# A memory-attention and mixture-of-experts kernel: copies moved to ScalarE, background work in one more place of each step, and two earlier loads of the last weights

## The chip, the cores and the metric

One core of one Trainium2 chip. The metric is the device time of one execution in microseconds (us); lower is better. The kernel before took 598.34 us (median of three executions, 596.36 to 599.28). Differences of up to about 0.5% are what such a measurement can't tell from no change.

## The reference

Inputs are float32: q, k, v of 4 batches x 8 heads x 576 tokens x 64, phi with 32 memory slots, weights of a dense mixture of 4 experts (w1 512x1024, w2 1024x512 each) and of a soft mixture of 8 experts with 4 slots each (called v1 and v2 in the kernel, phi2 for the slots).

```python
a = softmax(phi, axis=tokens)                       # 576 tokens -> 32 memory slots, per head
k_m, v_m = a.T @ k, a.T @ v                         # 32 x 64 per head
x = softmax(q @ k_m.T / 8, axis=-1) @ v_m           # -> (2304, 512)
p = domain_probs / domain_probs.sum(-1)
x = sum_e p[:, e] * (relu(x @ w1[e]) @ w2[e])       # 4 experts, all tokens
logits = x @ phi2                                   # (2304, 32)
d = softmax(logits, axis=0); c = softmax(logits, axis=1)
slots = d.T @ x                                     # 32 slots x 512
out = c @ (relu(slots_e @ v1[e]) @ v2[e] for 8 experts)   # (2304, 512)
```

## The kernel before, in words

The order of all instructions is written by hand: each engine executes its queue in the order in which the Python code issues them. The name in front of an arrow is the tile that an instruction writes, the names behind it are what it reads.

**Units and steps.** A unit is one batch (the last batch is cut in two). A unit has 8 steps n, one for each half of an expert's w1. A step has 8 products `up` (4 blocks fb x 2 halves ki of the tokens): 6 matmuls into one of two banks `mm` (L434 to L436, hi and lo parts of A and g), a relu by ScalarE into `hT` (L444) and, after the second half, a transposition by VectorE into `h` (L446). A holds the attention weights in two parts, hi and lo; g is w1 with v_m multiplied in (`g_mult`, L391), hi part by ScalarE (L401), lo part by VectorE (L402), one step ahead. `logits` (L461) multiplies hT by M, which is w2 @ phi2. So that w2 need not be applied per token, M is made in unit 0: in each step four `flip`s (four transpositions of a 128x512 piece of w2 into a bank, L488, copied out in two halves, L493 and L494), `part` (L500, L505) and `fold` (L510, copied to M at L514).

**The order within a step.** After each product comes a place, `at` = 0 to 7. `logits` of the step before stand at `at_l` = 0, `g_mult` of the next step at `at_g` = 2, its two output halves at `at_c` = 3 and 4. At all places but `at_g`, `pump` takes one entry from the list fg (softmax statistics, the token sums L625, row softmax of the unit before) and one from the list bg (`attention` of the next batch); an entry in `heavy` keeps bg waiting. In the first step of unit 0 the list `early` still finishes the attention of batch 0.

**`attention(b)`** lists loads and stages: kvs[0], kvs[1] (VectorE maxima of phi, L159), kvs[2] (transposes of them, L172), kvs[3] (subtractions), kvs[4] (exp on ScalarE), kvs[5], kvs[7] (VectorE sums, L207), kvs[6], kvs[8] (k times a), kvs[9] (the sums' matmuls, L243), kvs[10] (kbd, the blocks of keys, L266), kvs[11], kvs[12], kvs[13] (v times a), and for each of five token tiles scores (L315), exp, normalisation (L335 to L338) and transposition into A (L346 to L352). `shares` (L821, 20 small copies at L826 and L830) spreads domain_probs into `pe`.

**The end.** 160 blocks of 256 KB (32 of w2, 64 of v1, 64 of v2) pass through buffers that the main part no longer needs: `fill` loads n blocks into one buffer of a pool, `done` loads the next ones when they are used up. All loads are issued by SyncE, in order, about 8 in flight. Buffers: 5 blocks in those of the attention, 9 in each of five `big`, 4 each in A0, A1, two `raw`, two `g`. `raw`, one `g` and A0 hold h of the last unit until the last token sums (L625) are done.

Of the kernel before, what the change touches and what calls it, by code (L numbers as in the profile page):

```python
# [16 lines left out]
def kernel(  # L17
# [66 lines left out]
    vb = [const.tile([128, 128], F32, name=f"vb{n}") for n in range(2)]  # L84
    M = const.tile([128, 4 * NCH, NSLOT], F32)
    srun = const.tile([128, 8, 4, 32], F32)
# [62 lines left out]
    def kv_stages(b):  # L149
# [110 lines left out]
        def s5():  # L260
            t4 = bank()
            nc.tensor.transpose(
                t4[:, 0:128], st["km"].rearrange("p c d -> p (c d)"), ident
            )
            for c in range(2):
                nc.vector.tensor_copy(  # L266
                    out=kbd[b % 2][64 * c:64 * c + 64, :, c, :],
                    in_=t4[64 * c:64 * c + 64, 0:128].rearrange("p (i m) -> p i m", i=4),
                )
# [196 lines left out]
    def m_stages(n):  # L466
# [13 lines left out]
        def flip(a):  # L480
            def g():
# [11 lines left out]
                nc.scalar.copy(out=dst[0], in_=src[:, 0:2])  # L493
                nc.vector.tensor_copy(out=dst[1], in_=src[:, 2:4])  # L494
            return g
# [11 lines left out]
        def fold():  # L507
            t = bank()
            for a in range(4):
# [3 lines left out]
                )  # L513
            nc.vector.tensor_copy(  # L514
                out=M[:, 4 * n:4 * n + 4], in_=t[:, 0:128].rearrange("p (a s) -> p a s", a=4)
# [7 lines left out]
    def group(u):  # L523
# [69 lines left out]
        def weights(h):  # L593

            def f():
# [3 lines left out]
                we = st["we", h] = pc.tile([128, nt, 2, 32], F32, tag="we", bufs=2, name="we")  # L599
                for e in range(2):  # L600
                    nc.vector.tensor_tensor(
                        out=we[:, :, e], in0=st["dt"], in1=share(2 * h + e), op=ALU.mult
                    )
                if h == 1:
# [134 lines left out]
    with tc.manual_schedule():  # L739
# [96 lines left out]

        def pump():


            f = fg.pop(0) if fg else None  # L840
            if f:
                f()
            if f in heavy:
                return
            f = bg.pop(0) if bg else None
            if f:
                f()

        def attention(b):

# [9 lines left out]
            def with_q(f, m):  # L860
# [4 lines left out]
                return g  # L865
            items = [lambda: (load_phi(b), load_kv(b, 0)), lambda: load_kv(b, 1), kvs[0], kvs[1]]
            items += [kvs[2], None, kvs[3], lambda: load_q(b, 0), kvs[4]]
            items += [lambda: (load_q(b, 1), kvs[6]()), kvs[5], kvs[8], kvs[7], kvs[9], kvs[11], kvs[10]]
            items += [with_q(qs[0][0], 2), kvs[12], None, kvs[13]]
            for t in range(5):  # L870
# [14 lines left out]
        def finish(lu, n):  # L885
# [13 lines left out]
            if lu < NU - 3:  # L899
                bg.extend([None] * 8 + attention(lu + 2))  # L900

        for n, us in steps:
# [14 lines left out]
            if us == (0,) and n == 0:  # L917
                bg += attention(1)
                bg.insert(8, shares)
            if n == 0 and us[0]:  # L920
# [9 lines left out]
            if us == (NU - 2,) and n == NCH - 1:  # L930
                fill(bigp, "big", 9)
            if us == (NU - 1,) and n == MIX:
                for _ in range(4):
                    fill(bigp, "big", 9)
            gs = []
            for at, (u, fb, ki) in enumerate(ups):
                up(u, n, fb, ki)
                if at in at_c and gs:
                    gs.pop(0)()
                if at == at_l:  # L940
                    for lu, ln in last:
# [5 lines left out]
                if at == at_g and s + 1 < NG and us != (NU - 1,):  # L947
                    gs = g_mult(s + 1)
                else:
                    pump()  # L950
                if us == (0,):
# [11 lines left out]
        groups[lu][0](ln // 2)  # L963
        fill(const, "A1", 4, again=False)

        g_ = groups[lu][1]
# [7 lines left out]
        for _ in range(2):  # L974
            fill(rawp, "raw", 4)
        for _ in range(2):
            fill(gp, "g", 4)
        fill(const, "A0", 4, again=False)
# [242 lines left out]
```

## Time and profile before

| What | Value |
|---|---|
| Times of three executions | 599.28, 598.34, 596.36 us |
| The profiled execution's own time | 600.98 us |
| Its span | 599.1 us |
| Mean granted TensorE clock | 0.981 |
| TensorE matmul busy | 551.8 us (92%) |
| VectorE busy | 313.4 us (52%) |
| ScalarE busy | 204.2 us (34%) |
| Bytes moved by DMA | 106.22 MB |

Busy time is an average over stages. From about 40 to 505 us the four batches run through TensorE; from about 505 us on the blocks of the last weights stream in. Idle time of an engine counts only where the next step waits for it; "issue" as a releaser means that the profile shows none.

### The profile page before, as it was taken

To read this page: it belongs to the slowest core of one execution; us is meant where nothing else is said; L and a number is where in the kernel's file an instruction comes from. 1 tells how busy PE (TensorE), PEld (TensorE's weight loads), DVE (VectorE), ACT (ScalarE), POOL (GpSimd) and SP (SyncE) were. 2 spreads that over 40 slices of the span, in tenths; PEclk is the share of its full clock that TensorE was granted. 3 is DMA by queue.
4 is the path that set the end of the run, shared out by engine and by line. 5 is a ranking of instruction groups with operands and counts; after the bars stand their busy time and mean duration, and the time that the engine had idled before them with its cause. 6 is when DMAs were issued, how large, how long until landed. Compare 5 with 4: busy or idle time off the path is not lost.

```text
span 599.1 us, 15721 instructions
## 1 busy us (share of the span) xinstructions
PE 551.8 (92%) x6810; PEld 390.6 (65%) x6810; DVE 313.4 (52%) x693; ACT 204.2 (34%) x509; POOL 28.3 (5%) x34
## 2 busy tenths in 40 slices
PE   8887999999999899999989999999989998999993
PEld 7675778777776668877657787766557685324342
DVE  5656646864581566677345677761567362012022
ACT  2332445444451244554123344530444130102022
POOL 0000000101000001100000101000010000000000
PEclk9989999999999889999998899999999999999998
DMA  8992455444141733332446232440550398999998
GB/s 216 317 317 72 159 160 167 142 141 142 71 148 46 234 94 102 102 124 71 121 132 197 81 105 72 130 170 4 174 196 0 120 369 300 361 355 388 360 352 279
DMA packets 92771, 106.22 MB, mean 177 GB/s; under 512 B 30752, under 2 KB 55840, under 8 KB 92704
## 3 DMA queue, kind: packets, MB, share of 16 engines
q1 hardware_dynamic: 92704, 105.24, 54.2%
q8 instruction: 53, 0.87, 0.6%
q14 instruction: 14, 0.11, 0.1%
HBM read 100.50 MB, written 4.72 MB: 176 GB/s over the span
## 4 chain that ended last, share of the span: by engine, by line
PE 65%; DVE 14%; DMA 11%; issue 4%; ACT 3%; SPq 1%; POOL 0%; ACTq 0%; DVEq 0%; POOLq 0%
PE mm L434 11%; DMA v<-in_moe_w_dram 11%; PE at L625 9%; PE mm L436 9%; PE mm L435 9%; PE lb L461 6%; PE at L391 5%; DVE g L402 3%; PE at L315 3%; DVE h L446 2%; PE at L488 2%; PE mm L767 2%; PE at L299 1%; PE at L223 1%; ACT hT L444 1%
## 5 line engine op out<-in xcount | busy, mean ns | idle before, releaser
L444 ACT ACTIVATE hT<-mm 128x288 f32<-128x288 f32 x256 | 105.1, 411 | 235.0 <-PE mm L436 204.2
L446 DVE STREAM_TRANSPOSE h<-hT 128x576 f32<-128x576 f32 (+1 forms) x160 | 104.0, 652 | 138.6 <-ACT hT L444 126.8
L434 PE MATMUL mm<-A,g 128*128 128x288 f32 x512 | 170.4, 333 | 2.1 <-ACT g L401 1.0
L436 PE MATMUL mm<-A,g 128*128 128x288 f32 x512 | 153.2, 299 | 2.6 <-DVE g L402 2.6
L435 PE MATMUL mm<-A,g 128*128 128x288 f32 x512 | 152.6, 298 | 0.8 <-DVE A L352 0.8
L434 PEld LDWEIGHTS mm<-A,g 128*128 128x128 f32 x512 | 98.0, 191 | 48.9 <-ACT hT L444 20.4
L436 PEld LDWEIGHTS mm<-A,g 128*128 128x128 f32 x512 | 97.8, 191 | 3.9 <-DVE g L402 3.9
L435 PEld LDWEIGHTS mm<-A,g 128*128 128x128 f32 x512 | 98.3, 192 | 1.3 <-DVE A L352 1.0
L625 PE MATMUL at<-h,we 32*32 32x256 f32 x2304 | 58.3, 385 | 6.3 <-issue 4.4
L625 PEld LDWEIGHTS at<-h,we 32*32 32x32 f32 x2304 | 34.7, 103 | 25.5 <-issue 10.7
L402 DVE TENSOR_TENSOR g<-at,g 128x512 fp32r<-128x512 f32 x64 | 42.5, 671 | 5.5 <-ACT g L401 5.3
L461 PE MATMUL lb<-hT,M 128*32 128x288 f32 x512 | 40.8, 425 | 1.6 <-DVE M L514 1.6
L401 ACT CAST g<-at 128x512 fp32r<-128x512 f32 x64 | 37.2, 583 | 0.0
L391 PE MATMUL at<-raw,vb 64*32 64x512 f32 x512 | 36.5, 601 | 0.3 <-DVE srun L635 0.2
L1166 PE MATMUL mm<-v,hz 128*8 128x256 f32 x256 | 34.4, 380 | 0.6 <-DVE mm L1053 0.6
L1166 PEld LDWEIGHTS mm<-v,hz 128*8 128x8 f32 x256 | 13.3, 88 | 19.9 <-DMA v<-in_moe_w_dram 5.2
L488 PE MATMUL at<-ident,w 128*128 128x128 f32 x128 | 20.5, 284 | 3.3 <-issue 1.3
L461 PEld LDWEIGHTS lb<-hT,M 128*32 128x32 f32 x512 | 13.1, 111 | 15.0 <-issue 5.8
L541 DVE STREAM_TRANSPOSE lt<-lb 128x288 f32<-128x288 f32 x32 | 14.6, 470 | 14.6 <-PE lb L461 13.7
L1026 PE MATMUL mm<-v,sT 128*32 128x512 f32 x128 | 21.2, 597 | 0.9 <-DMA v<-in_moe_w_dram 0.5
L488 PEld LDWEIGHTS at<-ident,w 128*128 128x128 f32 x128 | 14.6, 143 | 10.6 <-issue 3.1
L552 POOL TENSOR_TENSOR lt<-lt,pe 128x576 f32<-128x576 f32 (+1 forms) x10 | 9.9, 989 | 226.3 <-DVE lt L541 226.3
(153 smaller groups left out, 523.7 us busy)
## 6 DMA issues: line engine op xcount, KB each, us to landing
v<-in_moe_w_dram SPq DMA_DIRECT2D x160, 256.0 KB, 5.7
raw<-in_moe_w_dram SPq DMA_DIRECT2D x32, 1024.0 KB, 5.1
w<-in_moe_w_dram SPq DMA_DIRECT2D x16, 512.0 KB, 6.9
kv<-in_k_dram SPq DMA_DIRECT2D x8, 512.0 KB, 4.8
kv<-in_v_dram SPq DMA_DIRECT2D x8, 512.0 KB, 6.1
out_dram<-ot SPq DMA_DIRECT2D x16, 256.0 KB, 4.1
q<-in_q_dram SPq DMA_DIRECT2D x12, 256.0 KB, 5.3
ph<-in_phi_dram SPq DMA_DIRECT2D x8, 256.0 KB, 5.6
```

What stands on the lines that cost most here:

```text
L391: nc.tensor.matmul(ts[c][32 * i:32 * i + 32, :], vb[b % 2][64 * c:64 * c + 64, 32 * i:32 * i + 32], raw[s][64 * c:64 * c + 64, i, :], star ...
L401: nc.scalar.copy(out=hi, in_=t)
L402: nc.vector.tensor_tensor(out=lo, in0=t, in1=hi.bitcast(F32), op=ALU.subtract)
L434: nc.tensor.matmul(ps, gh, ah, start=(c == 0), stop=False)
L435: nc.tensor.matmul(ps, gh, al, start=False, stop=False)
L436: nc.tensor.matmul(ps, gl, ah, start=False, stop=(c == 1))
L444: nc.scalar.activation(out=t[:, o0 - base:o1 - base], in_=ps, func=ACTF.Relu)
L446: nc.vector.transpose(out=hid[u, n // 2][:, :, 4 * (n % 2) + fb], in_=t[:, 0:o1 - base])
L461: nc.tensor.matmul(lb[u, ki][32 * a:32 * a + 32, 0:o1 - o0], M[:, 4 * n + a, :], hT[u, n, a][:, o0 - base:o1 - base], start=(f == 0), stop ...
L488: nc.tensor.transpose(t[:, 128 * c:128 * c + 128], st["w"][:, a, 128 * c:128 * c + 128], ident)
L625: nc.tensor.matmul(ts[p][32 * e:32 * e + 32, 0:256], st["we", e // 2][rows, tb, e % 2], hid[u, e][rows, tb].rearrange("p k f -> p (k f)"), ...
L1166: nc.tensor.matmul(accs[acc][32 * i:32 * i + 8, 0:256], hz[:, dh != 2, f, i, :], blk[:, 256 * m:256 * m + 256], start=(dh == 2 and f == 0) ...
```

## The change

The first unit's w2 copies (both halves), the copy into M and the copies into kbd are made by ScalarE. The two multiplications per half that make `we` become one instruction with the same elements. `pump` is called at `at_g` too, and takes from bg alone there. `attention` has a new order, and a number of empty places ahead of its first stage. `shares` moves from entry 8 to entry 3 of bg. In unit 0 both halves of g are put out at the first of the two places. One buffer `g` is filled with four blocks at the third step of the last unit, ahead of the four `big` ones, and M's buffer with two after the last logits.

```diff
@@ kv_stages, s5
-                nc.vector.tensor_copy(
+                nc.scalar.copy(
                     out=kbd[b % 2][64 * c:64 * c + 64, :, c, :],
@@ m_stages, flip and fold
                 nc.scalar.copy(out=dst[0], in_=src[:, 0:2])
-                nc.vector.tensor_copy(out=dst[1], in_=src[:, 2:4])
+                nc.scalar.copy(out=dst[1], in_=src[:, 2:4])
...
-            nc.vector.tensor_copy(
+            nc.scalar.copy(
                 out=M[:, 4 * n:4 * n + 4], in_=t[:, 0:128].rearrange("p (a s) -> p a s", a=4)
@@ group, weights
-                for e in range(2):
-                    nc.vector.tensor_tensor(
-                        out=we[:, :, e], in0=st["dt"], in1=share(2 * h + e), op=ALU.mult
-                    )
+                nc.vector.tensor_tensor(
+                    out=we, in0=st["dt"].unsqueeze(2).to_broadcast([128, nt, 2, 32]),
+                    in1=pe[:, b, tb0:tb0 + nt, 2 * h:2 * h + 2].unsqueeze(3).to_broadcast(
+                        [128, nt, 2, 32]
+                    ), op=ALU.mult,
+                )
@@ pump and attention
-        def pump():
+        def pump(both=True):
-            f = fg.pop(0) if fg else None
+            f = fg.pop(0) if fg and both else None
...
-            items = [lambda: (load_phi(b), load_kv(b, 0)), lambda: load_kv(b, 1), kvs[0], kvs[1]]
-            items += [kvs[2], None, kvs[3], lambda: load_q(b, 0), kvs[4]]
-            items += [lambda: (load_q(b, 1), kvs[6]()), kvs[5], kvs[8], kvs[7], kvs[9], kvs[11], kvs[10]]
-            items += [with_q(qs[0][0], 2), kvs[12], None, kvs[13]]
+            items = [lambda: (load_phi(b), load_kv(b, 0)), lambda: load_kv(b, 1)] + [None] * lead
+            items += [kvs[0], kvs[1], kvs[2], None, None, kvs[3], lambda: load_q(b, 0), kvs[4], kvs[5]]
+            items += [lambda: (load_q(b, 1), kvs[6]()), kvs[7], kvs[8], kvs[9], None, kvs[10]]
+            items += [kvs[11], with_q(qs[0][0], 2), kvs[12], None, kvs[13]]
...
-                bg.extend([None] * 8 + attention(lu + 2))
+                bg.extend([None] * 5 + attention(lu + 2, 5))
...
-                bg += attention(1)
-                bg.insert(8, shares)
+                bg += attention(1, 4)
+                bg[3] = shares
@@ the steps
             if us == (NU - 1,) and n == MIX:
+                fill(gp, "g", 4)
                 for _ in range(4):
                     fill(bigp, "big", 9)
...
                 if at in at_c and gs:
                     gs.pop(0)()
+                    if us == (0,):
+                        gs.pop(0)()
...
-                else:
-                    pump()
+                pump(not gs or at != at_g)
...
         fill(const, "A1", 4, again=False)
+        fill(const, "M", 2, again=False)
...
-        for _ in range(2):
-            fill(gp, "g", 4)
+        fill(gp, "g", 4)
```

**VectorE, first step of unit 0, from `at` = 2 on** (pe: the shares; w2T: a w2 flip; mx: the next batch's maxima; A: the attention weights). VectorE's queue at that place before:

```order
L402 TENSOR_TENSOR g<-at,g 128x512
L159 TENSOR_REDUCE mx<-ph 128x128
L352 TENSOR_TENSOR A_96<-at,A_96 128x2x128
L335 TENSOR_REDUCE asm<-ex 64x8
L336 TENSOR_SCALAR asm<-asm 64x8
L337 RECIPROCAL asm<-asm 64x8
L338 TENSOR_TENSOR ex<-ex,asm 64x256
L494 COPY w2T<-at 128x2x128 x2
L352 TENSOR_TENSOR A_96<-at,A_96 128x2x64
```

VectorE at the same place now:

```order
L402 TENSOR_TENSOR g<-at,g 128x512 x2
L828 COPY pe<-at 128x4x4 x4
L832 COPY pe<-at 128x2x4
L828 COPY pe<-at 128x4x4 x4
L832 COPY pe<-at 128x2x4
L828 COPY pe<-at 128x4x4 x4
L832 COPY pe<-at 128x2x4
L828 COPY pe<-at 128x4x4 x4
L832 COPY pe<-at 128x2x4
L352 TENSOR_TENSOR A_96<-at,A_96 128x2x128
L335 TENSOR_REDUCE asm<-ex 64x8
```

The second half of g and the 20 copies of the shares now stand ahead of the last normalisation of batch 0; the maxima and the w2 copies have left this place.

**VectorE, fourth step of unit 1** (sm: the next batch's sums over phi; lr, cmx: the row softmax; rs: the sums' result, from the matmuls L243). VectorE's queue in that step before:

```order
L402 TENSOR_TENSOR g<-at,g 128x512 x2
L647 TENSOR_TENSOR lr<-lr,cmx 128x576
L207 TENSOR_REDUCE sm<-ph 128x128
L446 STREAM_TRANSPOSE h<-hT 128x18x32
L207 TENSOR_REDUCE sm<-ph 128x128
L446 STREAM_TRANSPOSE h<-hT 128x18x32
L249 TENSOR_SCALAR rs<-at 128x2
```

VectorE in the same step now:

```order
L207 TENSOR_REDUCE sm<-ph 128x128
L446 STREAM_TRANSPOSE h<-hT 128x18x32
L402 TENSOR_TENSOR g<-at,g 128x512 x2
L649 TENSOR_TENSOR lr<-lr,cmx 128x576
L207 TENSOR_REDUCE sm<-ph 128x128
L446 STREAM_TRANSPOSE h<-hT 128x18x32
L249 TENSOR_SCALAR rs<-at 128x2
```

The first sum has moved ahead of both halves of g; the second one still stands right before the sums' matmuls.

**SyncE's loads of the last weights** (v: a buffer's blocks; x9 is a `big`, the first x9 the one filled in the half unit before). SyncE's queue there before:

```order
L690 DMA v_5705<-in_moe_w2_dram 128x512 x9
L690 DMA v_5767<-in_moe_w2_dram 128x512 x9
L690 DMA v_5777<-in_moe_w2_dram 128x512 x9
L693 DMA v_5787<-in_moe2_w1_dram 128x512 x9
L693 DMA v_5797<-in_moe2_w1_dram 128x512 x9
L693 DMA v_6283<-in_moe2_w1_dram 128x512 x4
L693 DMA v_6496<-in_moe2_w1_dram 128x512 x4
```

SyncE's queue at the same place now:

```order
L692 DMA v_5699<-in_moe_w2_dram 128x512 x9
L692 DMA v_5761<-in_moe_w2_dram 128x512 x4
L692 DMA v_5766<-in_moe_w2_dram 128x512 x9
L692 DMA v_5776<-in_moe_w2_dram 128x512 x5
L695 DMA v_5776<-in_moe2_w1_dram 128x512 x4
L695 DMA v_5786<-in_moe2_w1_dram 128x512 x9
L695 DMA v_5796<-in_moe2_w1_dram 128x512 x9
L695 DMA v_6280<-in_moe2_w1_dram 128x512 x4
L695 DMA v_6285<-in_moe2_w1_dram 128x512 x2
L695 DMA v_6494<-in_moe2_w1_dram 128x512 x4
```

Four blocks (v_5761) have moved ahead of the second `big`, and two (v_6285, in M's buffer) stand between A1's and the first `raw`.

## Rows read from the trace of the kernel before

**Rows 1.** The page, part 1: busy time of each engine, share of the span.

```profile
PE 551.8 (92%) x6810; PEld 390.6 (65%) x6810; DVE 313.4 (52%) x693; ACT 204.2 (34%) x509; POOL 28.3 (5%) x34
```

**Rows 2.** Timeline of TensorE, unit 0: start, us, instruction, [idle before <-releaser].

```profile
40.24 0.66 PE L488 MATMUL at<-ident,w 128*128 128x128 f32 x4 [1.05 <-DVE g L402]
...
43.48 0.40 PE L434 MATMUL mm<-A,g 128*128 128x288 f32 x1 [0.35 <-ACT A L351]
...
47.54 0.33 PE L172 MATMUL at<-ident,mx 128*128 128x128 f32 x1 [1.80 <-DVE mx L159]
...
57.43 0.63 PE L488 MATMUL at<-ident,w 128*128 128x128 f32 x4 [1.35 <-issue]
```

**Rows 3.** Waits of TensorE: line waited for, us in total, times, longest us.

```profile
PE lb L461 <- DVE M L514: 1.6, 2, 0.9
```

**Rows 4.** Groups by line, VectorE and ScalarE: busy us, mean ns | idle before.

```profile
L402 DVE TENSOR_TENSOR g<-at,g 128x512 fp32r<-128x512 f32 x64 | 42.5, 671 | 5.5 <-ACT g L401 5.3
...
L494 DVE COPY w2T<-at 128x256 f32<-128x256 f32 x32 | 13.2, 416 | 14.0 <-ACT w2T L493 13.9
...
L159 DVE TENSOR_REDUCE mx<-ph 128x128 f32<-128x512 f32 x8 | 8.0, 1012 | 1.4 <-DMA ph<-in_phi_dram 1.4
...
L826 DVE COPY pe<-at 128x16 f32<-128x16 f32 x16 | 1.6, 156 | 0.0
...
L444 ACT ACTIVATE hT<-mm 128x288 f32<-128x288 f32 x256 | 105.1, 411 | 235.0 <-PE mm L436 204.2 <-PE lb L461 26.3 <-DVE h L446 3.1
L401 ACT CAST g<-at 128x512 fp32r<-128x512 f32 x64 | 37.2, 583 | 0.0
L493 ACT COPY w2T<-at 128x256 f32<-128x256 f32 x32 | 12.2, 381 | 16.3 <-PE at L488 16.1
```

**Rows 5.** Stretches: busy us of PE, PEld, DVE, ACT, POOL; PEclk, DMA, GB/s.

```profile
60.00:165.00 105.00, 102.85 (x1021) 79.33 (x1020) 62.67 (x128) 50.09 (x127) 6.39 (x5) 1.00 0.42 140
204.00:208.00 4.00, 3.43 (x17) 3.43 (x18) 1.94 (x4) 0.61 (x2) 0.00 (x0) 0.57 1.06 363
221.00:225.00 4.00, 4.00 (x49) 2.75 (x52) 1.45 (x6) 0.41 (x1) 0.00 (x0) 0.57 0.02 4
```

**Rows 6.** Timeline of TensorE, unit 1.

```profile
200.07 0.30 PE L434 MATMUL mm<-A,g 128*128 128x288 f32 x1
...
200.87 0.29 PE L434 MATMUL mm<-A,g 128*128 128x288 f32 x1
...
203.05 0.33 PE L172 MATMUL at<-ident,mx 128*128 128x128 f32 x1 [1.11 <-DVE mx L159]
...
204.57 0.47 PE L172 MATMUL at<-ident,mx 128*128 128x128 f32 x1 [1.19 <-DVE mx L159]
...
220.67 0.38 PE L243 MATMUL at<-ind,sm 128*128 128x1 f32 x2 [0.93 <-DVE sm L207]
...
269.05 0.30 PE L346 MATMUL at<-ident,ex 64*128 64x64 f32 x2 [1.02 <-DVE ex L338]
```

**Rows 7.** The chain that ended last, in order of time: start, us, what.

```profile
96.56 0.44 PE at L488 x4
...
211.78 1.02 PE at L391 x16
```

**Rows 8.** Waits of SyncE's queue.

```profile
SPq L690 <- PE at L625: 34.6, 1, 34.6
...
SPq L693 <- PE at L625: 3.7, 1, 3.7
```

**Rows 9.** Stretches, last unit and end, columns as in Rows 5.

```profile
450.00:460.00 10.00, 9.07 (x75) 7.30 (x74) 7.54 (x18) 3.68 (x9) 0.00 (x0) 1.00 0.00 0
...
500.00:505.00 5.00, 3.01 (x88) 2.29 (x89) 1.01 (x3) 0.00 (x0) 0.00 (x0) 1.00 0.64 229
...
510.00:530.00 20.00, 18.78 (x160) 6.56 (x152) 3.68 (x16) 2.98 (x5) 0.00 (x0) 1.00 1.04 370
```

**Rows 10.** DMA issues: count, KB each, median us to landing.

```profile
v<-in_moe_w_dram SPq DMA_DIRECT2D x160, 256.0 KB, 5.7
```

More of the change, by code (lines that the diff above doesn't have):

```diff
@@ L84 @@
     vb = [const.tile([128, 128], F32, name=f"vb{n}") for n in range(2)]
-    M = const.tile([128, 4 * NCH, NSLOT], F32)
+    M = const.tile([128, 4 * NCH, NSLOT], F32, tag="M", name="M")
     srun = const.tile([128, 8, 4, 32], F32)
@@ L847, in pump, with attention @@
                 f()
-        def attention(b):
+        def attention(b, lead):
             kvs = kv_stages(b)
```

## The prediction, made before the changed kernel ran

> **What bounds the kernel now.** The page's first part comes first: TensorE's matmuls are busy for 551.8 us of a span of 599.1 [rows 1]. The change takes no matmul away, so it can gain only what TensorE loses: idle time (47.3 us in all), matmuls at half clock, and, at the end, waiting for data. The second view is the timeline of TensorE alone, read for the time in brackets, its idle time and who ended it. Unit 0 has four clear places in its first steps, at 40, 43, 47 and 57 us [rows 2], and two waits for M [rows 3]; from 60 to 165 us it loses only 105 - 102.85 = 2.15 us in all [rows 5]. Units 1 and 2 repeat one pattern: two waits for the maxima, one for the sums, one for the last normalised scores [rows 6]; the same four stand again 110.7 to 111 us later in unit 2, of the same size within 0.01 us. The third view is the granted clock by stretches: it falls to 0.50 for a part of 204 to 208 and of 221 to 225 us, right behind the first and the second of these groups [rows 5], and again in unit 2. A mean of 0.57 over 4 us is 4 x 0.43 = 1.7 us of work lost each time. The last view is the end: SyncE's queue stands for 34.6 us before a block of w2 [rows 8] while nothing moves from 450 to 460 us (0 GB/s), and from 510 us on DMA runs at its full share with 370 GB/s [rows 9]. The blocks set the pace there.
>
> **First steps of unit 0.** Ahead of the last normalisation of batch 0, VectorE now has the second half of g (0.67) and the 20 copies of the shares. Their 16 larger ones took 0.156 each but 1.6 together, since neighbours overlap: 0.10 each, 2.0 for 20; by single durations they would be 3.1. One maximum over phi (1.01) leaves the place [rows 4]. The fifth product waits for what this normalisation feeds, as it does now, at 43.48 [rows 2], so it comes 0.67 + 2.0 - 1.0 = 1.7 us later (2.8 at most). I take 1.7, because the busy time is what the queue really spends. Three waits have lost their cause: 1.80 for the maxima, which now start two products later and have `part` and `fold` to hide behind; 1.35 at 57.43, where flips stood behind banks that the shares' copies held; and the longer of the two waits for M (0.9), because M's copy now follows a relu on ScalarE and not the subtractions on VectorE. These are 4.05 us.
>
> What of the clock? There TensorE already idles 1.05 + 0.35 within 4 us without a fall; with 1.7 more it idles 3.1, and the nearest row is the pair of waits of 1.11 + 1.19 at 203 to 205, after which the clock fell [rows 5, 6]. I take the fall: 1.7. Sum of this place: 1.7 + 1.7 - 4.05 = -0.6, between -4.1 (no delay to speak of) and +1.6 (2.8 late, the fall, and one wait of 1.1 that stays).
>
> The Trainium skill, "TensorE: Matmul & The Clock Gate", on the HAM clock gate, has the same warning: half clock is the default and activity releases it, so idleness made in one place is paid for in the next. The fall at 204 agrees; the gaps at 47.54 and 57.43, without one, do not. Left out, the sum would be 1.7 lower.
>
> **The rest of unit 0.** ScalarE gets 32 copies of w2 that took VectorE 0.416 each; its own of the same shape take 0.381, so they don't become dearer [rows 4]. VectorE's waited 13.9 us for ScalarE's of the same bank, so the halves ran one behind the other anyway and the bank comes free no later. ScalarE's load from 60 to 165 us goes from 50.1 to about 50.1 + 28 x 0.4 + 2 = 63 us of 105: room on average. The order is what may hurt. After the fourth product of a step, ended at T, ScalarE's queue holds a relu (0.41), both casts of g (2 x 0.58) and two copies (0.8): T + 2.4, then the fifth product's relu, T + 2.8. Only two banks take products, so the seventh waits for that relu. It would start at T + 2 x 0.80 (two products start 0.80 apart [rows 6]) + two flips of 0.44 [rows 7] = T + 2.5. That is 0.3 a step, 2.1 in seven steps. Against it stand the second wait for M (0.7) and of the 2.15 us above some 1.2 that were waits for VectorE. Net +0.2. Ends: -2.1, if all of that idleness goes, and +13.3, if each of the 32 copies is paid in full. I take the value near the lower end because the stretch itself shows hidden copies (127 ScalarE instructions, hardly any idleness).
>
> **Units 1 and 2.** Maxima: VectorE's order after the token sums was h, g, mx, g, mx; it becomes mx, h, g, mx. The second maximum ends 1.01 + 0.67 earlier, and TensorE is there one product (0.80) earlier: 0.88 at most. I take 0.6, since neighbours overlap by 0.1 and more. Sums: the second sum no longer has the first one right ahead (1.0 and one transposition less, one half of g more), and the matmuls that wait for it come one product earlier: about 0.6 of the 0.93. Last scores: TensorE's own work between the normalisation and its transposes grows by the products of g (1.02 [rows 7]), which covers the wait of 1.02: 1.0. The background now takes 8 places a step and ends four places before the unit does; before it ended at its last place. Together 2.2 a unit, -4.4 for two; the ends are 0 (VectorE, denser now, is late by as much elsewhere) and -2 x (1.1 + 1.2 + 0.93 + 1.02) = -8.5, to which two falls of the clock may add 3.4. Since 1.7 of the pair of waits stays, I leave the falls in. K and v of the next batch are asked for a half step earlier, and SyncE then stands before w1 blocks; k and v wait for the same token sums as now, and the w1 block behind them is used some 10 us after their end: no cost.
>
> **The multiplications for `we`.** One instruction with the same elements stands where two stood, right after each other: 0, with nothing on either side that could move by more than one start of an instruction.
>
> **The end.** Up to the last token sums the buffers allow 5 + 9 + 36 + 4 = 54 blocks; all further ones wait for these sums (SyncE stands for 3.7 us, and DMA falls to 229 GB/s from 500 to 505 [rows 8, 9]). Now they allow 4 + 2 more. The four in `g` wait only for a product of the last unit's third step, so they load while the queue now stands. After the sums, 100 blocks are left for 106. A block of 256 KB (262,144 bytes [rows 10]) at 370 GB/s takes 0.71 us: 6 x 0.71 = -4.3. The ends are 0 (TensorE is the bound there) and -4.3. I take all of it, because there DMA is at its full share and TensorE is not.
>
> **Sum.** -0.6 + 0.2 - 4.4 + 0 - 4.3 = -9.1 us on the profiled execution's 600.98, which gives 591.9. That execution lies 2.6 above the median of the runs, so the median should be 598.34 - 9.1 = 589.2; I say 589.5.
>
> **Rivals.**
> *ScalarE's queue becomes the bound in unit 0 (slower).* The copies stand between relus in a queue that works in order, and each late relu holds one of two product banks. With every copy exposed, 32 x 0.416 = 13.3, the time is 598.3 - 0.6 - 4.4 - 4.3 + 13.3 = 602.3. It decides from 9.3 / 32 = 0.29 us a copy. For it: the burst at `at` = 3 of 2.4 us. Against it: 55 us of ScalarE's free time in that stretch.
> *The earlier blocks are hidden anyway.* If TensorE's own chain from the last sums to the output is as long as the stream, the 4.3 are lost: 593.8. For it: TensorE is busy for 18.78 of 20 us from 510 to 530. Against it: DMA is at its full share in the same stretch, and a matmul's modelled end can lie in a wait.
> *More goes than the waits themselves.* If the waits in units 1 and 2 become short enough that the clock holds at both sums (2 x 1.7), and the first step doesn't bring a fall (1.7), it is 589.2 - 5.1 = 584.1. The clock rule above leads here: each wait it calls for is paid twice.
>
> **How the numbers follow.** The forecast has 0.45, the hidden blocks 0.17, more than the waits 0.20, ScalarE's queue 0.18. What this kernel's measurement can tell from no change is about 0.5%, 3.0 us: 595.3 to 601.3. Faster: 0.42 + 0.12 + 0.20 = 0.74. The same: 0.03 + 0.05 + 0.06 = 0.14. Slower: 0.12. The range goes from 582 (the third rival with 2 us of its ends in units 1 and 2) to 600 (ScalarE's queue at four fifths of its price), which leaves some 0.1 on either side; the forecast's own goes from 586 to 594.
>
> **What will show it.** In the profile after: waits for M gone, none of 1.8 at the next maxima, but a longer wait before the fifth product and half clock at about 45 us; four waits in unit 1 that come to 2.0 in place of 4.25; no idle ScalarE-bound gaps in front of L434 between 60 and 165 us; DMA moving about 1 MB between 440 and 460 us, and the last block 9 us earlier than now. Wrong would be a TensorE that idles more than 5 us from 60 to 165 us, or an end that stays as long as it was after the last token sums.

## The result and the profile after

The changed kernel took 581.30 us (median of four executions, 576.26 to 581.74) beside 598.81 for the kernel before on the same chip: a ratio of 0.969, 95% interval 0.962 to 0.976, or 14.7 to 22.6 us less. It is faster, as forecast, but by about twice the 9.1 us of the sum, and 0.7 us under the low end of the range. A second measurement later (0.967, 0.963 to 0.971) agrees.

The profiled execution is the fastest of its four (576.26), and that of the kernel before was 2.6 above its median. So the two spans lie 24.8 us apart, and some 7 us of that is the choice of executions. The shape of the difference holds in all profiles below; its sum is read from the timed runs.

The first part of the changed kernel's page answers to [rows 1]:

```profile
PE 538.3 (94%) x6810; PEld 384.8 (67%) x6810; DVE 298.6 (52%) x635; ACT 216.0 (38%) x557; POOL 28.3 (5%) x34
```

The same 6810 matmuls are busy for 13.5 us less. By the stretches below, 7.7 of that lie in units 1 and 2, where the mean clock rose, and 5.0 in the end, where it didn't (0.97 and 0.95): there a matmul's modelled end can lie in a wait for a block, and fewer blocks were left to load. Of the kernel before (columns as in [rows 5]; 166.64 to 386.85 us are units 1 and 2, from 505.70 on the end after the last token sums, and 28 to 36 us the steps before batch 0's normalisation):

```profile
28.00:32.00 4.00, 2.78 (x13) 2.13 (x13) 2.48 (x8) 1.31 (x4) 0.00 (x0) 0.74 1.06 341
...
0.00:53.53 53.53, 44.09 (x456) 36.54 (x457) 32.27 (x87) 17.62 (x43) 1.20 (x8) 0.97 0.90 258
53.53:166.64 113.11, 109.61 (x1088) 84.12 (x1089) 65.66 (x151) 51.88 (x132) 6.39 (x5) 1.00 0.40 131
166.64:386.85 220.21, 209.56 (x2935) 159.65 (x2934) 133.66 (x260) 85.35 (x218) 12.82 (x10) 0.97 0.38 116
505.70:599.10 93.40, 79.55 (x540) 32.31 (x540) 18.25 (x51) 14.26 (x29) 0.52 (x1) 0.97 1.01 346
```

The same stretches of the changed kernel, between the same instructions:

```profile
40.00:44.00 4.00, 4.00 (x21) 3.85 (x22) 2.40 (x18) 1.67 (x5) 0.00 (x0) 0.57 1.07 359
...
0.00:51.42 51.42, 44.74 (x459) 37.30 (x459) 29.17 (x95) 19.21 (x49) 1.20 (x8) 0.97 0.92 263
51.42:162.03 110.61, 109.30 (x1087) 84.47 (x1087) 52.99 (x100) 61.12 (x170) 6.42 (x5) 1.00 0.42 136
162.03:368.66 206.63, 201.86 (x2935) 154.69 (x2934) 135.00 (x252) 86.23 (x222) 12.83 (x10) 1.00 0.40 123
486.36:574.30 87.94, 74.54 (x540) 31.11 (x540) 18.26 (x51) 14.26 (x29) 0.53 (x1) 0.95 1.02 353
```

Units 1 and 2 are the great part: 13.58 us less. Length less busy time gives TensorE's idleness, 10.65 before and 4.77 after: 5.9 us. The remaining 7.7 are busy time, at a mean clock of 0.97 before and 1.00 after: 0.03 x 220 = 6.6 us. Summed over fine stretches, the four places where the clock fell had lost 6.8 us (1.7 each), and after there is none. Two of the four are in [rows 5]; those of unit 2 lose 7 x 0.24 = 1.7 us each:

```profile
315.00:322.00 7.00, 6.68 (x46) 5.55 (x47) 4.49 (x9) 1.23 (x3) 0.00 (x0) 0.76 0.66 208
332.00:339.00 7.00, 7.00 (x94) 5.09 (x93) 2.89 (x9) 1.54 (x4) 2.60 (x2) 0.76 0.01 2
```

This is one execution. The profiles of the two experiments below that keep the order of before have three falls in units 1 and 2 (early loads alone) and two (ScalarE's copies alone). So 6.8 us is the most that any of these three executions lost to falls there.

TensorE's waits in unit 1 of the changed kernel, all there are above 0.2 us, answer to [rows 6] (unit 2 has 1.80 and 0.43 at the same places):

```profile
197.55 0.33 PE L172 MATMUL at<-ident,mx 128*128 128x128 f32 x1 [1.79 <-DVE mx L159]
211.48 0.38 PE L243 MATMUL at<-ind,sm 128*128 128x1 f32 x2 [0.43 <-DVE sm L207]
```

They come to 2.22 in place of 4.25, so the two units wait 4.1 us less at these places. Another 1.2 us of the 5.9 is one wait of unit 2 of the kernel before, at 293.71 ahead of the token sums (L625, "issue"), which is gone as well. In unit 0, against [rows 2], the wait for the shares' and g's chain is longer, and the waits of 1.80 for maxima and of 1.35 at a flip are gone; no wait for M is left [rows 3]:

```profile
38.85 0.44 PE L823 MATMUL at<-dp,rr 32*128 32x72 f32 x2 [1.33 <-DVE g L402]
...
44.95 0.40 PE L434 MATMUL mm<-A,g 128*128 128x288 f32 x1 [0.35 <-ACT A L351]
...
59.40 0.66 PE L488 MATMUL at<-ident,w 128*128 128x128 f32 x4 [0.32 <-DVE g L402]
...
75.84 0.66 PE L488 MATMUL at<-ident,w 128*128 128x128 f32 x4 [0.55 <-DVE g L402]
```

The groups by line answer to [rows 4]: ScalarE's copies are about as dear as VectorE's were, and the first matmuls of TensorE's products waited 0.3 us in all for a relu (L444):

```profile
L434 PE MATMUL mm<-A,g 128*128 128x288 f32 x512 | 168.5, 329 | 2.1 <-ACT g L401 1.0 <-ACT A L351 0.8 <-ACT hT L444 0.3
...
L494 ACT COPY w2T<-at 128x256 f32<-128x256 f32 x32 | 12.8, 399 | 0.0
```

At the end SyncE's one wait of 34.6 us [rows 8] has become two, of 18.6 before the four blocks in `g` and of 14.2:

```profile
SPq L692 <- PE mm L436: 18.6, 1, 18.6
...
SPq L692 <- PE at L627: 14.2, 1, 14.2
```

Stretches of the changed kernel around it answer to [rows 9]: DMA now moves 2.3 MB from 420 to 450 us (0.7 MB in the 30 us of the kernel before that answer to them, 440 to 470), and just before the last token sums it no longer sags to 229 GB/s.

```profile
420.00:430.00 10.00, 9.14 (x76) 6.33 (x75) 5.86 (x12) 5.07 (x12) 0.56 (x1) 1.00 0.34 127
430.00:440.00 10.00, 8.88 (x68) 7.13 (x67) 7.95 (x18) 3.62 (x9) 0.93 (x2) 1.00 0.09 25
440.00:450.00 10.00, 8.77 (x170) 6.27 (x168) 5.20 (x14) 2.72 (x9) 0.00 (x0) 1.00 0.24 82
480.00:485.00 5.00, 3.14 (x122) 1.92 (x106) 0.35 (x1) 0.00 (x0) 0.00 (x0) 1.00 1.02 369
```

### The profile page after: what moved, and what is told of

The parts are those of the page before. It is cut to its first block, busy times and chain, and to the rows that moved or that the text cites. A ratio compares the mean times of both kernels' runs of the same rounds, so it can differ in the third digit from the quotient of the medians.

```text
span 574.3 us, 15710 instructions
## 1 busy us (share of the span) xinstructions
PE 538.3 (94%) x6810; PEld 384.8 (67%) x6810; DVE 298.6 (52%) x635; ACT 216.0 (38%) x557; POOL 28.3 (5%) x34
## 4 chain that ended last, share of the span: by engine, by line
PE 71%; DMA 13%; DVE 8%; ACT 3%; issue 2%; SPq 1%; POOL 0%; ACTq 0%; DVEq 0%; POOLq 0%
PE mm L434 13%; DMA v<-in_moe_w_dram 12%; PE mm L436 10%; PE mm L435 10%; PE at L627 9%; PE lb L461 6%; PE at L391 5%; PE at L315 3%; PE at L488 3%; DVE g L402 2%; DVE h L446 2%; PE mm L769 2%; DMA out_dram<-ot 2%; PE at L223 1%; PE at L500 1%
## 5 line engine op out<-in xcount | busy, mean ns | idle before, releaser
L444 ACT ACTIVATE hT<-mm 128x288 f32<-128x288 f32 x256 | 106.1, 415 | 208.9 <-PE mm L436 174.3
L434 PE MATMUL mm<-A,g 128*128 128x288 f32 x512 | 168.5, 329 | 2.1 <-ACT g L401 1.0
L436 PE MATMUL mm<-A,g 128*128 128x288 f32 x512 | 151.6, 296 | 2.6 <-DVE g L402 2.6
L435 PE MATMUL mm<-A,g 128*128 128x288 f32 x512 | 151.0, 295 | 0.8 <-DVE A L352 0.8
L434 PEld LDWEIGHTS mm<-A,g 128*128 128x128 f32 x512 | 96.5, 188 | 48.0 <-issue 26.0
L436 PEld LDWEIGHTS mm<-A,g 128*128 128x128 f32 x512 | 96.2, 188 | 3.9 <-DVE g L402 3.9
L435 PEld LDWEIGHTS mm<-A,g 128*128 128x128 f32 x512 | 96.7, 189 | 1.3 <-DVE A L352 1.0
L627 PE MATMUL at<-h,we 32*32 32x256 f32 x2304 | 55.8, 385 | 4.9 <-issue 2.2
L627 PEld LDWEIGHTS at<-h,we 32*32 32x32 f32 x2304 | 33.7, 103 | 22.6 <-issue 7.3
L461 PE MATMUL lb<-hT,M 128*32 128x288 f32 x512 | 39.5, 413 | 0.0
L315 PEld LDWEIGHTS at<-kbd,qt 128*128 128x128 f32 (+1 forms) x160 | 17.8, 180 | 7.0 <-issue 3.9
L315 PE MATMUL at<-kbd,qt 128*128 128x64 f32 (+1 forms) x160 | 19.6, 266 | 0.2
```

What stands on the lines that cost most here:

```text
L315: nc.tensor.matmul(sc[0:n, :, j, :], st["qt"][:, j, 0:n], kbd[b % 2][:, j], start=True, stop=True)
L434: nc.tensor.matmul(ps, gh, ah, start=(c == 0), stop=False)
L435: nc.tensor.matmul(ps, gh, al, start=False, stop=False)
L436: nc.tensor.matmul(ps, gl, ah, start=False, stop=(c == 1))
L444: nc.scalar.activation(out=t[:, o0 - base:o1 - base], in_=ps, func=ACTF.Relu)
L461: nc.tensor.matmul(lb[u, ki][32 * a:32 * a + 32, 0:o1 - o0], M[:, 4 * n + a, :], hT[u, n, a][:, o0 - base:o1 - base], start=(f == 0), stop ...
```

## The experiments

Ratios are to the kernel before, run in the same job, with 95% intervals.

| Run | Median, us | Before, us | Ratio |
|---|---|---|---|
| early loads alone | 593.72 | 598.15 | 0.992 (0.989 to 0.995) |
| ScalarE's copies alone | 596.58 | 598.15 | 0.998 (0.995 to 1.001) |
| new order alone | 584.42 | 598.15 | 0.976 (0.972 to 0.980) |
| changed, copies back | 579.94 | 598.15 | 0.968 (0.965 to 0.972) |
| dummies, all units | 599.33 | 601.16 | 0.998 (0.995 to 1.001) |
| changed, second sum late | 580.61 | 601.16 | 0.969 (0.964 to 0.973) |
| changed, shares at entry 9 | 578.12 | 601.16 | 0.963 (0.960 to 0.967) |
| changed, empty places moved | 579.94 | 601.16 | 0.967 (0.963 to 0.970) |
| dummies, units 1 and 2 | 592.41 | 599.95 | 0.987 (0.983 to 0.991) |
| changed, as it is | 579.81 | 599.95 | 0.967 (0.963 to 0.971) |
| shares and empty place | 573.71 | 599.95 | 0.957 (0.954 to 0.961) |
| and g early in units 3, 4 | 572.27 | 599.95 | 0.955 (0.951 to 0.959) |

The theory: half of the gain is the new order's waits, and as much again is TensorE's clock, which had fallen because of those waits. The main rivals: the loads or ScalarE's copies bring it.

**Early loads alone**: the kernel before with the two early fills (and a tag for M, by which its buffer can be filled).

```diff
+                fill(gp, "g", 4)
                 for _ in range(4):
                     fill(bigp, "big", 9)
...
+        fill(const, "M", 2, again=False)
-        for _ in range(2):
-            fill(gp, "g", 4)
+        fill(gp, "g", 4)
```

> The kernel before with nothing but the two earlier loads (four blocks into a buffer g at the third step of the last unit, two into M's buffer). Theory (the end is paced by DMA): six blocks fewer after the last token sums, 6 x 0.71 = 4.3 us faster, some 594.5, and up to 5.5 if the last stretch also follows (the profile after shows the end 5.4 us shorter). Rival (TensorE's own chain is as long): the same time as before, within 1 us.

Measured: 4.7 us less (2.8 to 6.6). The wait in SyncE's queue split as in the changed kernel, and DMA no longer sagged before the sums:

```profile
SPq L690 <- PE mm L436: 18.7, 2, 18.4
...
SPq L690 <- PE at L625: 14.6, 1, 14.6
```

```profile
450.00:460.00 10.00, 9.08 (x71) 7.52 (x70) 7.50 (x19) 3.69 (x9) 0.00 (x0) 1.00 0.31 104
...
500.00:505.00 5.00, 4.52 (x99) 3.47 (x99) 1.89 (x6) 0.31 (x1) 0.00 (x0) 1.00 0.99 335
```

The end was bound by the stream of blocks; the rival of hidden blocks falls.

**ScalarE's copies alone**, in the kernel before:

```diff
-                nc.vector.tensor_copy(out=dst[1], in_=src[:, 2:4])
+                nc.scalar.copy(out=dst[1], in_=src[:, 2:4])
```

(and so for the copies into M and kbd.)

> The kernel before with nothing but the copies on ScalarE (second halves of the w2 flips, M, kbd). Theory (relieving VectorE is what shortened unit 0): unit 0 gives back most of the 4.6 us by which its end came earlier, 594 to 596, and the waits for M and the maxima in its first steps are gone. Rival (the order did it): 0 to 1 us faster, with the wait of 1.8 us for the maxima still there. Second rival (ScalarE's queue becomes the bound): slower by some us, with idle time in front of products between 60 and 165 us.

Measured: 1.4 us less (from 3.2 less to 0.4 more), which can't be told from nothing. TensorE's two waits for M are gone in its profile; those of 1.80 for the maxima and of 1.35 at a flip stand as before, so it is the order that removes these. The profile places a small gain in the rest of unit 0, 110.94 us in place of 113.11:

```profile
52.47:163.41 110.94, 109.31 (x1090) 84.01 (x1090) 54.46 (x116) 61.31 (x170) 6.41 (x5) 1.00 0.41 133
```

**New order alone**: `pump(both)`, `attention`'s new order and empty places, the shares at entry 3, both halves of g at the first place in unit 0; all of it stands in the diff of the change.

```diff
+        def pump(both=True):
+            f = fg.pop(0) if fg and both else None
...
+                pump(not gs or at != at_g)
```

> The kernel before with nothing but the new order (attention's list with its empty places, the extra place for background work, the shares earlier, both halves of g at once in unit 0); copies and loads as before. Theory (the order removes the waits and with them the falls of the clock in units 1 and 2): units 1 and 2 shorter by 6 to 7.5 us each as in the profile after, so 583 to 587 in all. Rival (only the waits, with the clock still falling): 2.5 to 3.5 us for each of the two units, 591 to 594.

Measured: 14.1 us less (11.7 to 16.5). Units 1 and 2 are as short as in the changed kernel, at full clock, to within 0.8 us:

```profile
166.67:374.10 207.43, 202.04 (x2934) 154.68 (x2933) 136.47 (x260) 85.30 (x218) 12.83 (x10) 1.00 0.40 123
```

**The changed kernel with the copies back on VectorE**: the reverse of the second experiment's edit.

```diff
-                nc.scalar.copy(out=dst[1], in_=src[:, 2:4])
+                nc.vector.tensor_copy(out=dst[1], in_=src[:, 2:4])
```

> The changed kernel with the copies (w2 second halves, M, kbd) back on VectorE, the rest as changed. Theory (with the new order VectorE has a place for them): within 1 us of the changed kernel, some 581. Rival (the copies on ScalarE are what makes unit 0 shorter): 3 to 5 us slower than the changed kernel, 584 to 586, all of it before the end of unit 0.

Measured: 0.968, the ratio of the changed kernel. So the order brings most, the loads 4 to 5 us, and ScalarE's copies perhaps 1 or 2 that these runs don't resolve.

**Dummies in all units.** The next question is whether idleness makes the clock fall. In the kernel before, TensorE gets work in its waits:

```diff
+                for _ in range(8 if b else 0):
+                    nc.tensor.matmul(t1[:, 384:512], ident, ident, start=True, stop=True)
...
+                for _ in range(6 if b and c else 0):
+                    nc.tensor.matmul(t3[:, 384:512], ident, ident, start=True, stop=True)
```

> The kernel before, order and copies untouched, with matmuls that nothing reads (eight 128x128 ahead of each transposition of the maxima, six ahead of the second of the sums' matmuls, batches 1 to 3), so that TensorE works through most of the waits while the waits themselves stay. Theory (the falls of the clock in units 1 and 2 come from these waits' idleness): the granted clock holds at 1.00 from 204 to 208 and from 221 to 225 and in unit 2, up to 4 x 1.7 us faster, 592 to 595, with units 1 and 2 at some 105.5 to 107.5 us each. Rival (the clock falls for another reason, or the new order's gain is in the waits alone): the clock still falls at these places, 0 to 2 us slower than before.

The time is 599.33, no change, and there is no usable profile: the profiled execution took 1657.88 us with TensorE busy for 99% of it, while the eleven others took 597.59 to 601.20. But the mean clock of each execution is on record: 0.987 to 0.996 in these eleven, and 0.977 to 0.985 in the seventeen of the kernel before. So the clock did hold better, and the time didn't gain by it. The dummies were too long, and stood in unit 0 too, where the clock didn't fall at these places; the next run with dummies leaves unit 0 out.

**The changed kernel with the second sum late** (the order of these two stages as before):

```diff
-            ... kvs[6]()), kvs[7], kvs[8], kvs[9], None, kvs[10]]
+            ... kvs[6]()), kvs[8], kvs[7], kvs[9], None, kvs[10]]
```

> The changed kernel with one pair of stages in attention's list swapped back (kvs[8] ahead of kvs[7]), so that the second sum again stands close ahead of the matmuls that wait for it. Theory (each wait is paid once as idleness, and again where the clock falls behind it): the wait grows from 0.43 to 1.1 to 1.3 us in units 0 to 2, at least 1.4 us in units 1 and 2 together and up to 3.4 more if the clock falls there: 582 to 586. Rival (VectorE has room in the new order): the wait stays under 0.6 and the time within 1 us of the changed kernel.

Its timeline in unit 1 and the clock of two stretches:

```profile
215.29 0.38 PE L243 MATMUL at<-ind,sm 128*128 128x1 f32 x2 [1.08 <-DVE sm L207]
```

```profile
214.00:218.00 4.00, 2.92 (x18) 2.67 (x18) 2.58 (x6) 1.36 (x3) 0.00 (x0) 0.84 0.04 9
218.00:222.00 4.00, 4.00 (x64) 2.13 (x63) 1.22 (x4) 1.34 (x4) 1.01 (x1) 0.73 0.00 0
```

With the wait back at 1.08 the clock falls again behind it: 4 x 0.16 + 4 x 0.27 = 1.7 us, in unit 2 too. But the profiled execution was the longest of its six (585.39 against 577.50 to 582.04), and the median is that of the changed kernel. So the profile shows the mechanism, and the time doesn't confirm its price: the mean clock was 0.979 in it and 0.985 to 0.991 in the others, so probably not every execution has these falls.

**The changed kernel with the shares at entry 9:**

```diff
-                bg[3] = shares
+                bg[9] = shares
```

> The changed kernel with the shares' entry at place 9 of the background list (second step of unit 0) in place of 3 (first step). Theory (in the first step the shares delay the fifth product and bring the fall of the clock there): the fifth product starts at 43 to 43.5 in place of 44.95, no half clock between 40 and 50 us in most executions, and a wait of 1 to 1.4 us behind the shares in the second step: 0 to 2 us faster. Rival (the shares are hidden in the first step, since VectorE stood idle there): no earlier fifth product, and 1 us or more slower.

The fifth product starts at 41.14 in place of 44.95, and the clock holds; the wait of 1.35 at a flip, which the kernel before had [rows 2], is back, now that the shares stand in the second step:

```profile
38.27 0.66 PE L488 MATMUL at<-ident,w 128*128 128x128 f32 x4 [1.05 <-DVE g L402]
...
41.14 0.40 PE L434 MATMUL mm<-A,g 128*128 128x288 f32 x1 [0.35 <-ACT A L351]
...
51.80 0.63 PE L488 MATMUL at<-ident,w 128*128 128x128 f32 x4 [1.35 <-issue]
```

```profile
40.00:44.00 4.00, 3.43 (x27) 2.83 (x29) 1.74 (x4) 1.09 (x3) 0.00 (x0) 1.00 1.08 360
```

In the timed runs this is 0.963 beside 0.967 for the changed kernel, whose intervals overlap. In the profiles the first steps are 3.8 us shorter (47.62 in place of 51.42) and the rest of unit 0 is 2.0 longer (112.56 in place of 110.61), so what is left is a gain that the timed runs don't resolve. The fall itself does belong to the shares' place: of the six profiles with the shares at entry 3 five have half clock between 38 and 47 us, and of the three with them at entry 9 none has.

**The changed kernel with the two empty places ahead of the transposition** of the maxima:

```diff
-            items += [kvs[0], kvs[1], kvs[2], None, None, kvs[3], ...
+            items += [kvs[0], kvs[1], None, None, kvs[2], kvs[3], ...
```

> The changed kernel with the two empty places moved ahead of kvs[2] (the transposes of the maxima), so that TensorE reaches them two products later. Theory (the 1.8 us wait there is for VectorE's second maximum and needs only more products ahead): the wait is gone in units 1 and 2, 3 to 3.6 us faster than the changed kernel, some 577.5. Rival (the subtractions behind it, now one place and not three after the transposes, become what TensorE waits for at the products of k): the wait moves to L185 or L223 and the time stays within 1 us.

The wait of 1.79 shrank to 0.27, and 1.01 turned up one stage later, at the next thing that needs VectorE:

```profile
199.39 0.33 PE L172 MATMUL at<-ident,mx 128*128 128x128 f32 x1 [0.27 <-DVE mx L159]
201.53 0.52 PE L185 MATMUL at<-ident,mb 128*128 128x128 f32 x3 [1.01 <-DVE mb L178]
```

The time stayed (0.967).

**Dummies in units 1 and 2 only**, 7 ahead of each transposition of maxima and 6 ahead of the second sums matmul, in the kernel before:

```diff
+                for _ in range(7 if b > 1 else 0):
+                    nc.tensor.matmul(t1[:, 384:512], ident, ident, start=True, stop=True)
...
+                for _ in range(6 if b > 1 and c else 0):
+                    nc.tensor.matmul(t3[:, 384:512], ident, ident, start=True, stop=True)
```

> The kernel before, with dummy 128x128 transpositions put into the waits of units 1 and 2: 7 ahead of each transposition of maxima and 6 ahead of the second sums matmul, some 0.7 to 0.8 us each, where it idled 1.11, 1.19 and 0.93. Nothing is waited for later or earlier than before; only TensorE works where it idled. Theory (the clock falls because of this idleness): the granted clock stays at 1.00 in units 1 and 2, the waits with the dummies in them stay as long as they were, and units 1 and 2 lose 3.4 us each, 6.8 in all: about 591 to 593. Rival A (the falls have another cause, such as the new order's density or the transfers): the clock falls as before, time 598 to 600. Rival B (the clock holds, but what was done late for the clock is hidden by something else): no falls and the same time.

Measured: 592.41, a ratio of 0.987, or 5.5 to 10.1 us less. TensorE's timeline in unit 1 (L173 and L246 are the dummies, here with 14 and 12 records) and the stretches, which answer to those of [rows 5] and to 166.64:386.85 above:

```profile
202.29 1.72 PE L173 MATMUL at<-ident 128*128 128x128 f32 x14
203.85 0.27 PE L174 MATMUL at<-ident,mx 128*128 128x128 f32 x1
...
219.21 1.58 PE L246 MATMUL at<-ident 128*128 128x128 f32 x12
220.63 0.28 PE L247 MATMUL at<-ind,sm 128*128 128x1 f32 x2
```

```profile
204.00:208.00 4.00, 4.00 (x36) 4.00 (x35) 2.78 (x6) 0.82 (x2) 0.00 (x0) 1.00 1.07 373
...
221.00:225.00 4.00, 4.00 (x73) 3.20 (x73) 1.54 (x5) 0.86 (x3) 1.13 (x1) 1.00 0.00 0
...
167.18:380.89 213.71, 210.72 (x3015) 163.72 (x3014) 133.98 (x260) 85.34 (x218) 12.85 (x10) 1.00 0.39 119
```

I had sized the dummies at 0.7 to 0.8 us a group; from start to start they take 1.56 and 1.42. They are longer than the waits that they fill (1.11, 1.19, 0.93), by 1.3 us a unit, and yet the two units are 6.5 us shorter, since the clock stays at 1.00. Nothing else was changed. That shows that TensorE's idleness at these places was what let the clock fall, and that the four falls of the profiled execution cost about 7 us.

How much it is in the timed runs can be estimated from the mean clock of each execution: the span times (1 - clock) is the work lost to half clock. On average the kernel before lost 11.0 us, this run 7.1 and the changed kernel 6.0 (8.7 in the four executions of the first measurement). These figures take in the end, where half clock may cost nothing, so they are rough; but by them some 4 of the 7.5 us here, and some 5 of the changed kernel's 20, are the clock. What the rest of this run's gain is stays open; in its profile units 3 and 4, which have no dummies, are 2.5 us shorter (116.37 in place of 118.85). So the theory holds in kind and not in size: the clock is about a quarter of the changed kernel's gain, and not as much as the waits.

The first try fits this, as an estimate. Its executions lost 4.9 us to half clock on average, and the kernel before 11.6: 6.7 less. A dummy takes 0.22 to 0.24 us by the rows above, so 8, 8 and 6 of them take about 5.0 a unit, 1.8 more than the waits in units 1 and 2 and 3.2 more than the one of 1.80 in unit 0: 6.7 in all. The overlong dummies ate what the clock gave back.

**The changed kernel, as it is**, in the same job, without an edit.

> The changed kernel as it is, in the job of the others: 580 to 582, ratio 0.969 to the kernel before; no fall of the clock in units 1 and 2 in its profile, at most one before the first logits. It measures how far two executions of it lie apart and serves as the base of the two variants.

579.81, 0.967; no fall in units 1 and 2, one at about 38 to 44 us.

**Shares at entry 9 and one more empty place** between the maxima and their transposition:

```diff
-            items += [kvs[0], kvs[1], kvs[2], None, None, kvs[3], ...
+            items += [kvs[0], kvs[1], None, None, kvs[2], None, kvs[3], ...
...
-                bg[3] = shares
+                bg[9] = shares
```

> The changed kernel with the shares in entry 9 (no fall of the clock in the first step and no late fifth product) and one more empty place between the maxima and their transposition (wait of 1.8 for the maxima gone in units 1 and 2). Theory: the waits for the maxima go without a new one, since the empty place is taken from behind the transposition: -1.8 per unit, and -2 to -3 in the first step: 575 to 577, some 4 to 6 us under the changed kernel of the same job. Rival: the wait turns up again one stage later (at the subtraction's VectorE result, 1.0 as with the two empty places ahead of the transposition), and only the shares' 2 to 3 us are gained: 578.

573.71: 6.1 us under the changed kernel, and the intervals are apart. The wait for the maxima is down to 0.27 and none stands one stage later; unit 1 pays 1.35 and unit 2 1.28 once for a w1 block, and the two units take 205.25 in place of 206.63:

```profile
195.74 0.33 PE L172 MATMUL at<-ident,mx 128*128 128x128 f32 x1 [0.27 <-DVE mx L159]
202.19 1.09 PE L391 MATMUL at<-raw,vb 64*32 64x512 f32 x16 [1.35 <-DMA raw<-in_moe_w_dram]
```

```profile
160.07:365.32 205.25, 201.31 (x2934) 154.41 (x2933) 133.82 (x252) 86.71 (x222) 12.81 (x10) 1.00 0.41 124
```

That is 1.4 of the 6.1. The profiled execution of the changed kernel was here again the fastest of its six, that of this run was the slowest of its six, and the two profiled spans lie only 1.7 apart (574.9 and 573.2). By the mean clocks another 1.2 us is half clock (4.8 us lost in place of 6.0); where the rest lies stays open.

**And g early in units 3 and 4**, where the changed kernel's TensorE waits for g, as in these rows of it:

```profile
417.96 0.40 PE L436 MATMUL mm<-A,g 128*128 128x288 f32 x1 [1.17 <-DVE g L402]
424.31 0.40 PE L436 MATMUL mm<-A,g 128*128 128x288 f32 x1 [0.81 <-DVE g L402]
```

```diff
-                    if us == (0,):
+                    if us == (0,) or n >= MIX and us[0] >= NU - 2:
                         gs.pop(0)()
```

> As the run with both edits, and both halves of g also put out at the first place in the two halves of the last unit, where TensorE waits 0.98, 1.17 and 0.81 us and three times 0.2 for g. Theory: these waits go with the first place, -1 to -3 us more than the run with both edits. Rival: the second half of g then stands ahead of relus and transpositions in ScalarE's and VectorE's queues, as it does in unit 0, and the products wait for these: 0 to +2.

572.27, the fastest of all, but its interval overlaps with the run before it. The two waits went and the one of 0.98 for ScalarE's half of g stayed; a smaller one, for a relu, came:

```profile
424.97 0.40 PE L434 MATMUL mm<-A,g 128*128 128x288 f32 x1 [0.54 <-ACT hT L444]
```

## Why the prediction was right in its waits and wrong in its size

| Step | Predicted | Profiles, before to after |
|---|---|---|
| First steps of unit 0 | -0.6 | 53.53 to 51.42: -2.1 |
| Rest of unit 0 | +0.2 | 113.11 to 110.61: -2.5 |
| Units 1 and 2, waits | -4.4 | idle 10.65 to 4.77: -5.9 |
| Units 1 and 2, clock | 0 | four falls of 1.7 to none: -6.8 |
| Units 3 and 4 | no term | 118.85 to 117.70: -1.2 |
| The end | -4.3 | 93.40 to 87.94: -5.5; alone -4.7 (2.8 to 6.6) |

**The step that failed** is the sentence "Since 1.7 of the pair of waits stays, I leave the falls in". The waits themselves came out as sized: 1.7 left at the maxima (measured 1.79), about 0.3 at the sums (0.43), none at the last scores: 4.1 us less in two units, where the sum had 4.4. What failed was to take the pair 1.11 + 1.19, with a fall behind it, as the measure for one wait of 1.8, and to keep the falls behind the sums' waits too, though these were to shrink to a third. The sum has two falls going at its far end, and none in the forecast; the runs show all four gone. The better row was in the same trace: 1.80 at 47.54 us, alone, with no half clock behind it [rows 2]. The third rival, "more goes than the waits themselves" (584.1, a chance of 0.20), came nearest. The run with dummies in units 1 and 2 shows its mechanism, since only TensorE's idleness differs there. But the rival had the clock hold behind the sums alone (2 x 1.7), and it held behind the maxima too. Its other half, that the first step brings no fall, didn't hold: half clock stands at 40 to 44 us (0.57).

**First steps.** The delay was right: the fifth product came at 44.95, 1.47 later (1.7 predicted), with the forecast fall ahead of it, and the three waits went. What the sum missed is that the kernel before already had a fall nearby, at 28 to 36 us, which the profile of the changed kernel doesn't have; this is the 1.5 between -0.6 and -2.1. Other profiles of either order show that fall or don't, so it isn't the change's.

**Rest of unit 0.** The 0.3 us a step for the seventh product didn't come: TensorE's first matmuls of a product (L434) waited 0.3 us for relus in the whole run. I had added single durations on ScalarE. Its timeline in a step of the changed kernel shows that neighbours start well before the one ahead has ended:

```profile
108.91 0.42 ACT L493 COPY w2T<-at 128x256 f32<-128x256 f32 x1
109.17 0.43 ACT L494 COPY w2T<-at 128x256 f32<-128x256 f32 x1
109.44 0.48 ACT L444 ACTIVATE hT<-mm 128x288 f32<-128x288 f32 x1
109.74 0.48 ACT L330 ACTIVATE ex<-ex 128x256 f32<-128x256 f32 x1
110.05 0.43 ACT L493 COPY w2T<-at 128x256 f32<-128x256 f32 x1
```

They are 0.26 to 0.31 apart where each takes 0.42 to 0.48. So 48 more copies made ScalarE busy for 216.0 - 204.2 = 11.8 us more, 0.25 each. For VectorE's 20 small copies I had used the busy time for that very reason, and not for ScalarE. The first rival, ScalarE's queue as the bound, falls with this.

**The end** was right in place, cause and size.

**The multiplications for `we`** were costed at nothing and not tried alone. In the timed runs the parts come to 14.1 + 4.7 + 1.4 = 20.2 us beside 17.5 and 20.1 measured, which leaves nothing of size to look for there.

**The sum.** In the timed runs, the order's 14.1 us against 5.0 forecast for it (0.6 + 4.4) is the whole miss, 9.1 us. An estimate splits it. By the mean clocks of the executions, the work lost to half clock went from 10.2 us to 7.1 with the new order alone, 3.1 less, where the sum had one fall more, 1.7: that is 4.8 of the 9.1. The other half is idleness: in the profile of that run 1.5 us more than forecast in units 1 and 2, 1.0 in the rest of unit 0 (112.13 in place of 113.11) and 1.4 in units 3 and 4 (117.43 in place of 118.85), which the forecast took as unchanged by the order.

## What to carry to other kernels

Where the clock falls behind a wait, add the half clock to the cost of the wait, and ask what remains after the change whether it looks like waits behind which the trace shows a fall or like those without; put both answers into the sum's range. To prove a clock effect, fill the wait with dummy work that is no longer than the wait, and change nothing else; to size it, take the mean clock of all executions, since one profile can have four falls and the next one two. And size a queue's burst from the starts of neighbours in the timeline, not from the sum of their durations.

## What the runs showed of the hardware

Single waits of 1.79 and 1.80 us left the clock at 1.00 (units 1 and 2 of the changed kernel), while single ones of 0.93 and 1.08 ahead of the sums' matmuls had half clock behind them in all eight cases (two in each of three profiles with the order of before, and two with the second sum late). The pair of 1.11 and 1.19 (within 0.01) stood in the three former profiles six times, and half clock followed it three times. So the length of one idle stretch doesn't decide alone; what else does, these runs don't show. With the order of before and no dummies, the three profiles had nine falls in their six units 1 and 2; with the changed kernel's order or a variant of it, eight profiles had none in sixteen units, and the variant with the second sum late had two in two. The Trainium skill, "TensorE: Matmul & The Clock Gate", section "A second HAM failure mode: psum-queue depth-cycling", tells of a kernel in which short idleness between groups of matmuls, not one long wait, makes the clock swing; the pair, in the three cases with a fall, agrees with that.

One execution of one kernel took 1657.88 us, 2.8 times as long as its other eleven, with TensorE busy for nearly all of it and a recorded clock of 1.00 from 167 to 1200 us. Why isn't known.
